# Running the last six spectral modes after all the side work, instead of the last three

## The chip, the cores and the metric

The kernel runs on one core of one Trainium2 chip. The metric is the device time of an execution in microseconds (us), as a median over runs. PE is TensorE, DVE is VectorE, ACT is ScalarE, POOL is GpSimd, SP is SyncE; PEld is the weight load of PE. Times of 0.2% matter in this case, so every variant was timed in five rounds beside the kernel before.

## The reference, cut to what matters

```python
x = attention(q, k, v)                     # 8 batches x 576 rows x 512 columns; half local, half strided heads
X = np.fft.rfft(x, axis=1)                 # cut to 64 modes
Yr = Xr[m] @ w_r[m] - Xi[m] @ w_i[m]       # for each mode m, 512 x 512 weights
Yi = Xr[m] @ w_i[m] + Xi[m] @ w_r[m]
y = np.fft.irfft(Y, n=576, axis=1)
u = x + y
out = u + np.maximum(u @ w_ch, 0.0)        # the channel mix
```

The weights of the modes are 64 x 2 x 1 MB in float32, some 134 MB of the 163 MB that the kernel reads. They are cast to float16 on the way in.

## The kernel before: the parts that matter

The modes run twice over, once for each half of the channels. The second pass, `mode(1, m)`, has "pieces" of other work set between its modes: turns (transposes of the attention's output) and premixes (x @ w_ch, and x put into row order). A `spec` turns the spectra of sixteen finished modes through w_ch. The instructions of PE run in the order in which they are written.

```python
def mode(slot, m):                          # 16 matmuls of 128x128 by 128x16
    ...
    for e in range(4):
        for c in range(4):
            nc.tensor.matmul(yv[:, mi, e, :], wt[pr, XC[c], ds(128 * e, 128)],
                             Xh[half][pr, c, :, :, m], start=(c == 0), stop=(c == 3))
    if m % 2 and (slot or m // 2 not in GUEST):
        w_fetch()                           # a free buffer: the next two modes' weights
    ends = {7: 8}
    if slot and mg == 7:
        ends = {5: 6, 7: 2}                 # the last eight modes are added up as 6 + 2
    ...                                     # after mode 61 and after mode 63: YT = yp + Y0 on DVE
```

```python
work = [...]                                # 4 turns of w_ch, then for each batch 4 turns and 5 premixes: 76
LATE = 10
first = len(work) - 2 * LATE
for m in range(NM - 3):                     # modes 0 to 60
    mode(1, m)
    if m < NM - 3 - LATE:
        upto = -(-first * (m + 1) // (NM - 3 - LATE))
    else:
        upto = first + 2 * (m - (NM - 4 - LATE))     # two pieces a mode
    for w in work[n:upto]:
        w()
    n = upto
    if m >= 16 and m % 16 in (4, 8):
        spec(m // 16 - 1, 0 if m % 16 == 4 else 1)

psum_pools(v=3, u=3)                        # the banks of the pieces become those of the channel mix
...
for i in range(3):                          # five early passes, 512 columns each
    if i < 2:
        v_early(i)
    u_early(i)
warm = psum("v")

def again(n):                               # filler: a matmul whose result nobody reads
    for i in range(n):
        nc.tensor.matmul(warm, idn, v0s[0][:, 2, :], start=True, stop=True)

for m in range(NM - 3, NM):
    mode(1, m)
again(2)
spec_last(0)                                # needs YT of modes 62 and 63: the tail starts here
again(3)
...                                         # v_rows, u_rows for 36 units of 128 rows, and the output
```

The softmax here doesn't subtract the row's maximum and nothing guards it: scores larger than these inputs give would overflow.

## Time and profile before

| what | before |
|---|---|
| time, median of three runs | 436.75 us (436.56 to 436.8) |
| span in the profile | 434.8 us |
| PE busy | 334.7 us, 77% |
| DMA, mean over the span (bytes counted after the cast to float16) | 212 GB/s |
| tail, from `spec_last` (398.0) to the end | 36.8 us |

Two rows of the page for the kernel before, its span in 40 equal slices: the granted clock of PE in tenths of full speed, and the GB/s moved.

```profile
PEclk9999899869895585988885559585769687999999
GB/s 174 210 212 213 214 212 213 211 210 212 214 214 212 214 213 214 214 213 214 214 213 213 213 213 214 214 214 213 213 213 214 213 213 215 213 176 13 268 316 287
```

The transfers run flat at 213 GB/s until slice 35, whatever the clock does: the kernel streams its inputs, weights above all, for 390 us. Slice 36 (391 to 402 us) moves 13 GB/s. There the weights are in and the first output isn't out. This gap is what the change is about.

### The profile page before, as it was taken

The page shows a single profiled execution, that of the slowest core. Times are in us where ns is not written, and L with a number is a line of the kernel's source. Part 1 is how long each engine was busy: PE and PEld are TensorE (multiplying, and loading weights), DVE is VectorE, ACT ScalarE, POOL GpSimd, SP SyncE. Part 2 cuts the span into 40 slices and gives each one's busy share as a digit, 9 for nine tenths or more (in the row PEclk, how much of TensorE's full clock was granted, in tenths as well). Part 3 has the DMA queues.
Part 4 walks back from the last instruction along what each step waited for, and adds up shares of the span by engine and source line. Part 5 has one row for each costly group of instructions (what it writes and reads, how often), then busy time and mean ns, then how long its engine had stood idle before and what let it go on. Part 6 is the DMA issues. An engine that isn't in the chain of part 4 may idle for free.

```text
span 434.8 us, 12063 instructions
## 1 busy us (share of the span) xinstructions
PE 334.7 (77%) x5289; PEld 241.1 (55%) x5289; DVE 215.0 (49%) x466; ACT 188.0 (43%) x353; POOL 129.3 (30%) x208
## 2 busy tenths in 40 slices
PE   1987988789876879787865567679596769888994
PEld 1865776667765666665753345445454445554442
DVE  2788788744452242442511034244335443764895
ACT  1587678635542433534440302113313312443883
POOL 6423332323232222222222222222222222200893
PEclk9999899869895585988885559585769687999999
DMA  8999999999999999999999999999999999980787
GB/s 174 210 212 213 214 212 213 211 210 212 214 214 212 214 213 214 214 213 214 214 213 213 213 213 214 214 214 213 213 213 214 213 213 215 213 176 13 268 316 287
DMA packets 28995, 92.16 MB, mean 212 GB/s; under 512 B 4048, under 2 KB 5072, under 8 KB 28944
## 3 DMA queue, kind: packets, MB, share of 16 engines
q0 software_dynamic: 24704, 81.28, 94.2%
q1 hardware_dynamic: 3440, 9.46, 5.8%
q10 hardware_dynamic: 800, 0.67, 0.6%
q8 instruction: 41, 0.67, 0.6%
q14 instruction: 10, 0.08, 0.0%
HBM read 163.22 MB, written 9.44 MB: 397 GB/s over the span
## 4 chain that ended last, share of the span: by engine, by line
DMA 73%; PE 19%; DVE 2%; issue 2%; ACT 1%; POOL 1%; DVEq 0%; POOLq 0%
DMA wt<-in_moe_w_i_dram 51%; DMA ring<-in_v_dram 7%; DMA ring<-in_k_dram 6%; DMA wt<-in_moe_w_r_dram 4%; DMA ring<-in_q_dram 4%; PE sc L645 3%; PE y L547 3%; PE v L688 2%; PE u L688 2%; PE v L890 2%; PE y L514 1%; PE tp L653 1%; DVE yy L678 1%; PE u L911 1%; DVE xT L597 1%
## 5 line engine op out<-in xcount | busy, mean ns | idle before, releaser
L547 PE MATMUL y<-X,wt 128*128 128x16 f16 (+1 forms) x2048 | 82.4, 192 | 63.5 <-DMA wt<-in_moe_w_i_dram 60.9
L547 PEld LDWEIGHTS <-wt 128*128 128x128 f16 (+1 forms) x2048 | 72.6, 103 | 75.6 <-issue 72.3
L196 POOL DMA_DIRECT2D wt<-in_moe_w_r_dram x62 | 36.5, 589 | 142.2 <-PE y L547 63.1
L196 POOL DMA_DIRECT2D wt<-in_moe_w_i_dram x60 | 35.4, 590 | 70.6 <-DMA wt<-in_moe_w_i_dram 57.9
L654 ACT ACTIVATE v<-sc 128x512 f16<-128x512 f32 x32 | 18.9, 597 | 86.1 <-PE sc L645 86.0
L645 PE MATMUL sc<-w_cp,xT 128*128 128x512 f16 (+1 forms) x160 | 51.3, 450 | 0.4 <-DVE xT L617 0.4
L471 ACT ACTIVATE PL<-sc 128x480 f16<-128x480 f32 (+1 forms) x48 | 27.6, 579 | 47.4 <-PE sc L457 46.9
L655 DVE COPY xo<-tp 128x512 f16<-128x512 f16 x32 | 22.1, 692 | 45.5 <-PE tp L653 45.5
L250 DVE TENSOR_TENSOR xb<-av,rec 90x256 f16<-90x256 f32 (+2 forms) x80 | 36.0, 450 | 2.8
L249 DVE RECIPROCAL rec<-av 90x4 f32<-90x4 f32 (+2 forms) x80 | 14.7, 183 | 42.1 <-PE av L486 31.3
L402 DVE COPY qT<-tp 128x576 f16<-128x576 f16 x16 | 12.0, 758 | 42.8 <-PE tp L395 39.4
L260 ACT ACTIVATE v<-tp 128x640 f16<-128x640 f16 (+1 forms) x24 | 19.4, 808 | 21.2 <-PE tp L429 17.8
L395 PE MATMUL tp<-cI_s,ring 64*64 64x64 f16 x864 | 26.4, 210 | 2.2 <-issue 1.4
L360 ACT ACTIVATE PL<-sc 90x360 f16<-90x360 f32 (+1 forms) x48 | 22.7, 490 | 5.6 <-PE sc L353 4.9
L922 DVE TENSOR_TENSOR osb<-u,rl 128x512 f32<-128x512 f32 x36 | 23.6, 688 | 2.6 <-PE u L688 1.3
L395 PEld LDWEIGHTS <-ring 64*64 64x64 f16 x864 | 20.6, 122 | 7.4 <-issue 4.4
L905 POOL TENSOR_TENSOR rl<-rl,xo 128x512 f32<-128x512 f32 x16 | 18.3, 1156 | 20.5 <-ACT rl L903 20.2
L441 PE MATMUL sc<-cMl_s,cI_s 128*128 128x480 f16 (+1 forms) x48 | 22.4, 467 | 1.6 <-ACT X L260 1.6
L260 ACT ACTIVATE kz<-tp 64x360 f16<-64x360 f16 (+1 forms) x32 | 19.0, 595 | 10.2 <-PE tp L395 8.6
L457 PE MATMUL sc<-qT,kz 128*128 128x160 f16 (+1 forms) x160 | 22.6, 267 | 0.2 <-issue 0.2
L645 PEld LDWEIGHTS <-xT 128*128 128x128 f16 (+1 forms) x160 | 14.5, 109 | 14.6 <-issue 5.7
L285 PE MATMUL tp<-cI_s,ring 72*128 72x72 f16 x256 | 15.1, 206 | 9.5 <-DMA ring<-in_v_dram 8.0
(103 smaller groups left out, 647.8 us busy)
## 6 DMA issues: line engine op xcount, KB each, us to landing
wt<-in_moe_w_r_dram POOLq DMA_DIRECT2D x62, 512.0 KB, 18.9
wt<-in_moe_w_i_dram POOLq DMA_DIRECT2D x60, 512.0 KB, 19.4
out_dram<-osb SPq DMA_DIRECT2D x14, 512.0 KB, 2.7
ring<-in_v_dram POOLq DMA_DIRECT2D x8, 288.0 KB, 13.4
ring<-in_q_dram POOLq DMA_DIRECT2D x8, 288.0 KB, 13.6
ring<-in_k_dram POOLq DMA_DIRECT2D x8, 288.0 KB, 13.2
ring<-in_v_dram POOLq DMA_DIRECT2D x3, 512.0 KB, 15.5
ring<-in_q_dram POOLq DMA_DIRECT2D x3, 512.0 KB, 14.9
```

The source lines that it names most:

```text
L196: nc.gpsimd.dma_start(dst, rows)
L250: nc.vector.tensor_tensor(out=dst, in0=val.rearrange("p h (q c) -> p h c q", c=4), in1=rec[0:n, 0:pieces] .to_broadcast((n, pieces, 64)) . ...
L260: nc.scalar.activation(out=out, in_=in_, func=ACTF.Copy)
L360: nc.scalar.activation(out=PS[0:n, ds(POFF[t], 4 * n)], in_=scp[0:n, 0 : 4 * n], func=ACTF.Exp, scale=SCALE,)
L395: nc.tensor.transpose(tp[ds(64 * hp, 64), ds(64 * i, 64)], qn[ds(64 * hp, 64), ds(64 * (9 * g + i), 64)], idn[ds(64 * hp, 64), ds(64 * hp, ...
L441: nc.tensor.matmul(scp[:, 0 : n * times].rearrange("p (h x) -> p h x", h=times), idn, mask_rows("cMl", n, times), start=True, stop=False,)
L457: nc.tensor.matmul(scp[:, ds(col, n)], kzs[par][:, hp, ds(s0, 128)], qTs[par][:, ds(s0, n)], start=False, stop=(i == len(todo) - 1),)
L471: nc.scalar.activation(out=dst, in_=src, func=ACTF.Exp, scale=SCALE)
L547: nc.tensor.matmul(yv[:, mi, e, :], wt[pr, XC[c], ds(128 * e, 128)], Xh[half][pr, c, :, :, m], start=(c == 0), stop=(c == 3),)
L645: nc.tensor.matmul(vp[pr, :], xT[:, ch, cols], w_chs["cp"][:, ch, :], start=(ch == 0), stop=(ch == 3),)
L655: nc.vector.tensor_copy(out=xo[pr].rearrange("p (h q c) -> p h q c", h=2, c=4), in_=tp[pr, 0:512].rearrange("p (h c q) -> p h q c", h=2, c=4),
L922: nc.vector.tensor_tensor(out=osb[:, t % 2, :], in0=up, in1=rls[b, t][:, t % 2, :], op=AluOp.add)
```

## The change

Its intent: the last six modes, not the last three, are freed of pieces, so that these modes can run as soon as their weights land; the early passes, which need no weights, go between them, and fillers keep PE going. To have all pieces out by mode 57, two pieces a mode begin earlier.

```diff
-    LATE = 10
+    LATE = 12
+    END = NM - 6
     first = len(work) - 2 * LATE
-    for m in range(NM - 3):
+    for m in range(END):
         mode(1, m)
-        if m < NM - 3 - LATE:
-            upto = -(-first * (m + 1) // (NM - 3 - LATE))
+        if m < END - LATE:
+            upto = -(-first * (m + 1) // (END - LATE))
         else:
-            upto = first + 2 * (m - (NM - 4 - LATE))
+            upto = first + 2 * (m + 1 - (END - LATE))
...
-    for i in range(3):
-        if i < 2:
-            v_early(i)
-        u_early(i)
-    warm = psum("v")
...
-    for m in range(NM - 3, NM):
+    early = [lambda i=i: v_early(i) for i in range(2)]
+    early += [lambda i=i: u_early(i) for i in range(3)]
+    warm = psum("v")
+    for m in range(END, NM):
         mode(1, m)
-    again(2)
+        if m < END + 2:
+            for w in early[3 * (m - END) : 3 * (m - END) + 3]:
+                w()
+        else:
+            again(3 if m < NM - 1 else 2)
     spec_last(0)
```

## The prediction

> **What bounds the kernel now.** I read four views in this order: the chain that ended last, cut to 364 to 400 us; the issues of weight transfers with their time to landing, one by one; the timeline of TensorE (PE) from 318 to 372 us; and busy time with granted clock by stretch. The chain comes first, because it says which wait ended last in the only stretch that the change touches, the passage from the second half of the spectral modes to the channel mix. Its columns are start, length and what.
>
> ```profile
> 350.00 18.91 DMA wt<-in_moe_w_i_dram
> ...
> 369.05 0.65 PE y L547 x16
> ...
> 393.02 0.24 PE tp L653 x4
> 393.26 0.02 issue
> 393.28 0.70 DVE xoh L655
> ...
> 394.03 0.39 PE v L890
> ...
> 395.28 0.49 PE y L547 x16
> ...
> 395.86 0.57 DVE YT L575
> ...
> 396.47 1.12 PE y L547 x32
> 397.59 0.43 PE v L952 x2
> 398.02 0.99 PE y L882 x4
> ```
>
> The last transfer on the chain lands at 368.9 us. It carries modes 52 and 53 (each fetch brings two modes, and groups of 16 matmuls of L547 counted back from the last one give the mode numbers). From there to the end the chain is work on the core, not DMA: pieces of turn (L591, L612) and premix (L645, L653), modes, two passes of spec, then the early passes (L890, L911), mode 61 at 395.28, and modes 62 and 63 from 396.47 to 397.59. `spec_last`, which opens the tail, starts at 398.02. So here PE is late. How late is told by the landings of the last two of the eight single-mode transfers, issued at 381.48 and 384.00 (columns: name, queue and operation, count, size, us to landing):
>
> ```profile
> wt<-in_moe_w_i_dram POOLq DMA_DIRECT2D x1, 256.0 KB, 11.7
> wt<-in_moe_w_i_dram POOLq DMA_DIRECT2D x1, 256.0 KB, 9.8
> ```
>
> They land at 381.48 + 11.7 = 393.2 (mode 62) and 384.00 + 9.8 = 393.8 (mode 63). By the same sum modes 58 and 59 are there at 364.34 + 19.4 = 383.7, mode 60 at 371.83 + 15.6 = 387.4 and mode 61 at 374.17 + 14.5 = 388.7. The kernel runs mode 58 at 384.99, 60 at 390.31, and 62 at 396.47: it is behind the weights by 1.3, 2.9 and 3.3 us. In this stretch it falls behind steadily, as it puts two pieces after each mode. That 3.3 us is nearly all that any reordering before the tail can win; it is 0.75% of 436.75.
>
> Then I looked for where PE has room earlier (timeline of PE; in brackets the idle time before and who ended it):
>
> ```profile
> 354.36 0.65 PE L547 MATMUL y<-X,wt 128*128 128x16 f16 x16 [2.41 <-DMA wt<-in_moe_w_i_dram]
> ...
> 359.21 0.64 PE L547 MATMUL y<-X,wt 128*128 128x16 f16 x16 [2.42 <-DMA wt<-in_moe_w_i_dram]
> 359.69 1.87 PE L645 MATMUL sc<-w_cp,xT 128*128 128x512 f16 x4
> ...
> 366.38 1.03 PE L645 MATMUL sc<-w_cp,xT 128*128 128x512 f16 x4
> ```
>
> Before modes 46 and 48 PE stands idle for 2.4 us each, waiting for weights, and afterwards the same four matmuls take 1.87 instead of 1.03 us until about 364.6. The stretches show the clock behind that (PE, PEld, DVE, ACT, POOL busy with counts; then granted clock, DMA share, GB/s):
>
> ```profile
> 351.00:353.00 2.00, 0.94 (x27) 0.80 (x23) 1.63 (x5) 0.00 (x0) 0.59 (x1) 1.00 1.08 217
> 357.00:359.00 2.00, 0.00 (x0) 0.00 (x0) 0.72 (x3) 0.00 (x0) 0.59 (x1) 0.50 1.04 211
> 361.00:363.00 2.00, 2.00 (x24) 1.23 (x23) 0.69 (x1) 0.60 (x1) 0.29 (x1) 0.50 1.05 211
> ```
>
> The clock is 0.50 there, while DMA stays at 211 to 217 GB/s whatever PE does.
>
> **What the Trainium skill says.** "TensorE: Matmul & The Clock Gate", Part 1, says that the array runs at half clock after an idle window of about 3.4 us and at full clock after a busy one. The trace agrees with the halving (0.50 against 1.00), though here a gap of 2.4 us next to sparse work was enough. Part 2 of that page says that matmuls stay in program order and only weight loads are pulled ahead; so a mode queued behind pieces waits for them even when its weights have landed, which the lags of 1.3 to 3.3 us show. "PSUM — Partial Sum Buffer", Terms, forbids two engines in one bank at once; the trace has mode 62 idle for 0.72 us until the add of modes 56 to 61 has left their bank. "DMA: Bandwidth & Descriptors", The descriptor swizzle, gives partitions 64 to 127 to half of the engines; the last transfers, the imaginary weights, go only there, and the DMA share falls from 1.07 to between 0.53 and 0.62 after 388 us. That fixes the landings; the change doesn't touch it.
>
> **The change part by part.** Pieces are the same 76, modes the same 64.
>
> *Moved: six pieces earlier.* By the old formula 58 pieces are done when mode 52 comes, by the new one 64; two after each mode now begin at mode 46, not 51, and all 76 are out after mode 57. A premix costs PE 0.86 + 0.22 = 1.08 us at full clock (chain, L645 and L653), a turn about 0.5 (L591 or L612), a mode 0.49. Between mode 46 and mode 52 come pieces 52 to 63, where it was 52 to 57 with only one turn before mode 48. The pieces now filling the waits are premixes 53 to 55 ahead of mode 48: 3 x 1.08 = 3.2 us at full clock against 2.42 us of idle.
>
> *End of the pieces.* Old: from mode 52 (369.05) to the last piece (393.26) PE takes 24.2 us, with hardly any DMA wait. New, counted from mode 46 (354.36): 24.2, less three modes that go behind the pieces (1.5), plus modes 46 to 51 (6 x 0.49 = 2.9), plus pieces 52 to 57 (0.5 + 5 x 1.08 = 5.9) makes 31.5, so 385.9 at full clock. The idle before mode 46 shrinks only by one turn, so I expect a cold stretch of 3 to 5 us still to follow it, which costs 1.5 to 2.5 us; the end is then near 388.
>
> *The last six modes.* From that end: mode 58 (0.49), beside which most of the 0.77 us wait for the last copy (393.26 to 394.03) passes, the rest 0.3; three early passes (0.65 at 0.22 each); mode 59 (0.49); two (0.43); mode 60 (0.49); three filler matmuls (0.65); mode 61 (0.49); three fillers (0.65, in place of the 0.72 us wait for the add). Sum 4.6: mode 62 could start at 392.6 if the pieces end at 388, at 390.5 if they end at 385.9. Either way its weights land only at 393.2. So modes 62 and 63 become bound by DMA.
>
> *Added on the path.* Mode 62 starts at 393.35 (mode 52 started 0.15 after its landing), ends at 393.84; three fillers take 0.65; mode 63, landed by then, ends at 394.98; two fillers 0.43: `spec_last` at 395.4. The nine new fillers are 9 x 0.22 = 2.0 us of PE, but six lie beside waits; three, 0.65 us, lie on the path. Removed from the path are 398.02 - 395.4 = 2.6 us. The tail, 434.8 - 398.0 = 36.8 us, has the same instructions. 436.75 - 2.6 = 434.15 if all goes well.
>
> **Rivals.**
> 1. *The crowded modes 46 to 57 push PE's lag on to the end.* If the cold stretch lasts until 364 as before, or turns (0.7 to 0.9 us of VectorE each) and the two specs (1.73 us of copies each) stall PE more closely packed, the pieces end at 389.5 and mode 62 starts at 394.1. For it: VectorE is already on the chain between 369.97 and 373.37. Against: those waits are in the 24.2 us already. It would leave 1.8 us of gain, 434.9.
> 2. *Idle before mode 62 cools the clock, and the tail starts at half speed.* If the pieces end at 385.9, PE waits up to 2.7 us less fillers' effect, the length that stood before the cold stretches. A cold stretch of 4 us in a tail where PE is busy 96% (9.64 of 10 us, 400 to 410) costs about 2 us: 436 to 437. Against: PE is dense up to that wait and the fillers stand on both sides of modes 61 to 63.
> 3. *Fetches go out later, as modes free their buffers later.* Mode 51 may be 2 us later. Against: these issues also wait for earlier transfers to complete, and 10 to 19 us lie between issue and landing; a delay of 2 us is absorbed. If not, landings slip by 1 us: 435.2.
> 4. *The last landing isn't the bound and the whole 3 us or more comes:* would need earlier landings; nothing moves bytes. 433.5.
>
> **Range and chances.** I take 434.4: the sum, with a little of rivals 1 and 2. Rival 4 gives the low side, 433.4; rival 2 most of the high side, 436.2. A gain of over 2% would be 8.7 us, more than twice the lag that can be recovered: 1%. A loss of over 2% needs several cold stretches or a broken DMA flow: 1%.
>
> **What would show each step.** Right: mode 62 waits for the imaginary weights near 393.2, that transfer joins the chain, `spec_last` starts near 395.4, the idle of 2.42 us before mode 48 is gone, and the tail still lasts 36.8 us. Wrong: PE has no DMA wait after mode 58 (rival 1); clock below 1.00 and L688 matmuls of twice the length after 394 (rival 2); last landings after 394.5 (rival 3); or the tail's length changes, for which I see no reason.

## The result, and the profile after

The changed kernel takes 434.65 us as a median of four runs (433.94 to 435.15), against 436.77 us (436.56 to 436.91) for the kernel before in the same rounds. The ratio is 0.9951, with a 95% interval of 0.9933 to 0.9968. The prediction was 434.4.

The profiled run took 434.99 us, with a span of 433.2 us. `spec_last` starts at 396.4 instead of 398.0, and the tail is again 36.8 us: all of the 1.6 us between the two traces was won ahead of the tail.

The chain that ended last, of the changed kernel (start, length, what):

```profile
386.51 0.58 ACT zz L260
...
388.92 0.60 ACT v L654
389.52 0.03 issue
389.54 0.60 ACT v0h L654
390.14 0.04 issue
390.19 0.59 PE v L891 x2
...
393.03 0.49 PE y L547 x16
...
393.61 0.57 DVE YT L575
394.18 0.04 issue
394.22 0.64 PE y L547 x16
...
396.42 0.99 PE y L883 x4
```

Modes 62 and 63 are still not on the chain by way of a transfer. Mode 62 at 394.22 waits for the add of modes 56 to 61 on DVE, as before. The last two transfers, issued at 382.25 and 384.70 in this trace, took:

```profile
wt<-in_moe_w_i_dram POOLq DMA_DIRECT2D x1, 256.0 KB, 10.8
wt<-in_moe_w_i_dram POOLq DMA_DIRECT2D x1, 256.0 KB, 9.6
```

So mode 62 was there at 393.05 and mode 63 at 394.3. They ran at 394.22 and 395.34: PE is 1.2 and 1.0 us behind its weights, where it had been 3.3 us behind. The timeline of PE tells where the last microsecond went:

```profile
355.07 0.64 PE L547 MATMUL y<-X,wt 128*128 128x16 f16 x16 [3.14 <-DMA wt<-in_moe_w_i_dram]
...
361.80 0.65 PE L547 MATMUL y<-X,wt 128*128 128x16 f16 x16
...
380.25 1.22 PE L645 MATMUL sc<-w_cp,xT 128*128 128x512 f16 x3 [0.81 <-DVE xT L617]
...
382.21 1.87 PE L645 MATMUL sc<-w_cp,xT 128*128 128x512 f16 x4
```

The lines are modes 46 and 48 and two premixes. Mode 48 (361.80) has no wait left, as foreseen; the wait before mode 46 (355.07) did not shrink but grew, from 2.41 to 3.14 us. Then a premix at 382.21 takes 1.87 us for its four matmuls, the half-speed figure, in a place where the kernel before ran at full clock. The same stretch in both kernels, first before, then after (PE, PEld, DVE, ACT, POOL busy with counts, granted clock, DMA share, GB/s):

```profile
380.00:385.00 5.00, 4.09 (x52) 2.71 (x51) 3.91 (x9) 2.25 (x4) 1.03 (x2) 1.00 1.06 211
```

```profile
380.00:385.00 5.00, 4.75 (x35) 2.53 (x36) 1.64 (x4) 1.19 (x2) 1.11 (x3) 0.66 1.06 211
```

The mean clock is 0.66 instead of 1.00, and PE gets 35 matmuls through in place of 52 (of another mix: the 52 hold more of the short transposes). The question for the experiments was whether the passage is bound by landings (theory A, the prediction) or by the core's own work (theory B, its first rival), and what the clock, the order of the modes and the fillers each do.

### The profile page after: what moved, and what is told of

Its sections match the earlier page's. It is cut to its first block, busy times and chain, and to the rows that moved or that the text cites. A ratio compares the mean times of both kernels' runs of the same rounds, so it can differ in the third digit from the quotient of the medians.

```text
span 433.2 us, 12081 instructions
## 1 busy us (share of the span) xinstructions
PE 337.0 (78%) x5298; PEld 241.4 (56%) x5298; DVE 215.6 (50%) x466; ACT 188.1 (43%) x353; POOL 129.2 (30%) x208
## 4 chain that ended last, share of the span: by engine, by line
DMA 59%; PE 26%; DVE 7%; issue 3%; ACT 3%; POOL 0%; DVEq 0%; POOLq 0%
DMA wt<-in_moe_w_i_dram 48%; DMA wt<-in_moe_w_r_dram 5%; PE y L547 4%; DMA ring<-in_q_dram 4%; PE sc L645 3%; DMA ring<-in_k_dram 2%; PE v L688 2%; PE u L688 2%; PE v L891 2%; PE tp L395 2%; PE sc L514 2%; DVE kz L292 1%; DVE xb L250 1%; PE sc L441 1%; DMA ring<-in_v_dram 1%
## 5 line engine op out<-in xcount | busy, mean ns | idle before, releaser
L645 PE MATMUL sc<-w_cp,xT 128*128 128x512 f16 (+1 forms) x160 | 52.8, 456 | 1.5 <-DVE xT L617 1.5
L655 DVE COPY xo<-tp 128x512 f16<-128x512 f16 x32 | 22.1, 692 | 31.9 <-PE tp L653 31.9
L597 DVE COPY xT<-tp 128x512 f16<-128x512 f16 x16 | 11.0, 689 | 25.6 <-PE tp L591 13.7
```

Of the source, the lines that this page charges most:

```text
L645: nc.tensor.matmul(vp[pr, :], xT[:, ch, cols], w_chs["cp"][:, ch, :], start=(ch == 0), stop=(ch == 3),)
L655: nc.vector.tensor_copy(out=xo[pr].rearrange("p (h q c) -> p h q c", h=2, c=4), in_=tp[pr, 0:512].rearrange("p (h c q) -> p h q c", h=2, c=4),
```

## The experiments

Twelve kernels. The first four ran on one chip (the kernel before: median 437.16 us, 11 runs), the other eight on another (437.01 us, 11 and 12 runs). The landings are worked out from issue and time to landing, as above.

| kernel | time, us | ratio to before | mode 62 landed / ran | mode 63 landed / ran | `spec_last` |
|---|---|---|---|---|---|
| before | 436.75 | 1 | 393.2 / 396.47 | 393.8 / after 62 | 397.98 |
| after | 434.65 | 0.9951 | 393.05 / 394.22 | 394.3 / 395.34 | 396.37 |
| a_again | 434.67 | 0.9938 | 392.9 / 396.26 | 394.1 / 397.38 | 398.36 |
| a_nofill | 435.59 | 0.9963 | 392.2 / 392.91 | 393.5 / after 62 | 394.98 |
| a_even | 435.31 | 0.9961 | 392.8 / 392.91 | 394.0 / 394.18 | 395.51 |
| a_pair | 434.07 | 0.9920 | 390.9 / 392.60 | 393.3 / 393.73 | 394.70 |
| b_old_warm | 437.92 | 1.0016 | 392.2 / 397.33 | 393.4 / after 62 | 398.84 |
| b_warm | 434.21 | 0.9940 | 392.7 / 392.83 | 393.9 / 394.06 | 395.09 |
| b_even_warm | 434.37 | 0.9936 | 392.5 / 392.61 | 393.6 / 393.79 | 394.81 |
| b_even_pair | 434.77 | 0.9945 | 391.5 / 391.60 | 394.0 / 394.14 | 395.17 |
| c_old_even | 434.99 | 0.9951 | 391.9 / 393.75 | 393.2 / after 62 | 395.51 |
| c_lump | 434.02 | 0.9930 | 393.1 / 393.77 | 394.3 / 394.89 | 395.87 |
| c_warm_pair | 433.66 | 0.9929 | 391.3 / 391.42 | 393.8 / 393.94 | 394.97 |
| c_whole | 435.16 | 0.9962 | 393.4 / 393.54 | 393.4 / 394.67 | 395.69 |

The traces are one execution each; the times are medians of five or six runs (of three before, four after), and the profiled run is one of those. All the ratios of variants that gained lie between 0.992 and 0.9963, with intervals of some 0.2% to either side, so most variants can't be told apart by time; the traces must do that. They have an offset of their own: mode 46's weights landed at 354.95 us in the changed kernel and at 354.24 in the kernel before, so differences of 0.7 us between absolute times of two traces mean little.

### a_again: the changed kernel once more

No edit.

> The changed kernel unaltered, for a second trace and as a measure beside its variants. Theory A (landing): modes 62 and 63 start when their imaginary weights land, near 393.1 and 394.3 us. Theory B (late core): the core's own work of pieces and specs reaches mode 62 after the landing; in the first trace it starts at 394.22 against a landing of 393.05. Under B this trace shows again some 1 us between landing and start, and the pieces end after 389; a cold stretch of the clock somewhere between 376 and 386 may be there or not. Time 434.65, within 0.6, ratio to before 0.995.

Measured: 434.67 us (433.92 to 436.97), ratio 0.9938 (0.9914 to 0.9963). The profiled run happened to be the slowest, 436.97 us. Its clock fell twice late, to 0.50 between 369 and 371 us and to 0.50 between 383 and 385, and mode 62 ran 3.4 us after its landing. Theory B holds, and the cold stretch at 380 to 386 was no accident of the first trace. In that run the gain was gone: `spec_last` started at 398.36, against 397.98 in the trace of the kernel before. When the clock falls differs from run to run, and in these two traces the time with it.

### a_nofill: the nine new fillers taken away

```diff
-            again(3 if m < NM - 1 else 2)
+            again(0 if m < NM - 1 else 2)
```

> The nine filler matmuls ahead of modes 61, 62 and 63 taken away, the two after mode 63 kept. Both theories have the landing of mode 63 (394.3) as the floor: spec_last can start at 394.3 + 0.15 + 0.49 + 0.43 = 395.4, against 396.42. Theory B: fillers cost what lies on the path, 0.65 ahead of mode 61 and 0.65 ahead of mode 63, but the landing caps the gain at 1.0 us: 433.6. Theory A in its strict form: only the 0.65 ahead of mode 63 is on the path: 434.0. Theory C (fillers keep the clock up): the granted clock falls below 1.00 between 394 and 402 and the time is 435.5 or more.

Measured: 435.59 us (434.71 to 437.71), ratio 0.9963. Up to `spec_last` the fillers do cost something: from mode 60 to `spec_last` it is 3.8 us (391.18 to 394.98), against 4.6 us (391.74 to 396.37) with them, so 0.8 us of the nine lie on the path. But `spec_last` itself:

```profile
394.98 1.91 PE L883 MATMUL y<-w_ch,YT 128*128 128x512 f16 x4
```

It takes 1.91 us instead of 1.04, and the clock is 0.72 from 393 to 395 and 0.50 from 395 to 397. From `spec_last` to the last matmul it takes 32.0 us (394.98 to 426.97) where the changed kernel takes 30.9 (396.37 to 427.23). This is what theory C expected, and the time of 435.59 agrees: the fillers give back 1.1 us in the tail for 0.8 us ahead of it. By time alone the two kernels aren't apart (434.67 in the same rounds, and the intervals overlap).

### a_even: pieces spread evenly

```diff
-    LATE = 12
+    LATE = 0
```

> LATE = 0: the pieces are spread evenly over modes 0 to 57 (1.31 per mode), none crowded late; 68 of 76 are done when mode 52 comes, instead of 64. Theory B: the core is no longer late, the pieces are all out by 388 and modes 58 to 63 wait for their weights; mode 62 starts within 0.3 us of its landing near 393.1, mode 63 follows after 0.65 of fillers at 394.3 or 394.5, spec_last near 395.5: 433.7. Theory A: the passage is bound by landings already, no gain: 434.6. Theory C: the idle time moves to the last modes, where it cools the clock: below 1.00 after 394 and 436.

Measured: 435.31 us (434.98 to 437.35), ratio 0.9961. The first half of theory B came true (mode 62 ran 0.1 us after its landing, `spec_last` started at 395.51), and the gain was eaten by what theory C had named (timeline of PE):

```profile
392.91 0.64 PE L547 MATMUL y<-X,wt 128*128 128x16 f16 x16 [2.39 <-DMA wt<-in_moe_w_i_dram]
...
395.51 1.91 PE L883 MATMUL y<-w_ch,YT 128*128 128x512 f16 x4
```

Here PE is on time: mode 62 waits for its transfer, and after that wait the clock is at 0.50 for the start of the tail, even with three fillers on each side. From `spec_last` to the last matmul it takes 31.7 us, 0.9 us more than in the changed kernel.

### a_pair: the last transfers in another order

```diff
+            if i >= 2 * NM - 4:
+                for j in range(2):
+                    for ri, src in enumerate((moe_w_r, moe_w_i)):
+                        nc.gpsimd.dma_start(wt[ds(64 * ri, 64), j] ..., src[m + j, ...] ...)
```

(in place of both real modes, then both imaginary ones.)

> The last two fetches in the order real 60, imaginary 60, real 61, imaginary 61, and so on, instead of both reals before both imaginaries: real weights go to partitions 0 to 63 and imaginary ones to 64 to 127, and in the old order the DMA share is halved for the last 6 us (387 to 393). If both halves of the engines finish together, the last landing comes about 3 us earlier, near 391. Theory B: modes start no earlier, since the core is late anyway: 434.6. Theory A: spec_last comes 1.0 us or more earlier (up to 3): 433.6 or less. If the landing doesn't move, the order of the issues isn't what spaces the last transfers.

Measured: 434.07 us (433.42 to 434.49), ratio 0.9920 (0.9901 to 0.9939). The last landing was at 393.3, not near 391: only mode 62 moved up, to 390.9. The DMA share fell to 0.54 between 389 and 391 us as before (0.54), so the uneven order isn't why the last transfers are slow. Mode 62 ran at 392.60, bound by the add once more, so landings weren't its limit here either; the time lies between what theories A and B expected. What sets this trace apart is that its clock didn't fall a second time:

```profile
380.12 0.82 PE L656 MATMUL sc<-w_cp,xT 128*128 128x512 f16 x3 [0.81 <-DVE xT L628]
...
381.48 1.03 PE L656 MATMUL sc<-w_cp,xT 128*128 128x512 f16 x4
...
384.74 0.64 PE L558 MATMUL y<-X,wt 128*128 128x16 f16 x16
```

The instructions from there to mode 57 are those of the changed kernel (lines shifted by 11). Here they take 4.6 us (380.12 to 384.74), there 6.1 us (380.25 to 386.31). A second cold stretch costs 1.4 us.

### b_old_warm: the kernel before, kept warm in its idle time

```diff
+        if m in {43: 4, 45: 8, 47: 8}:
+            fill({43: 4, 45: 8, 47: 8}[m])      # filler matmuls into an idle bank
```

> The kernel before, with 4, 8 and 8 filler matmuls after the pieces of modes 43, 45 and 47, where PE stands idle for weights anyway: 0.9 and 1.7 us each at full clock. Theory D: PE is late at the end because those idle times cool its clock (0.50 from 354.7 to 364.6, which costs some 4 us of PE); kept warm, it reaches modes 62 and 63 about 2 to 3 us earlier and the kernel before gains as much as the change does: 434 to 435. Theory E: the change gains by putting work into the idle time and modes behind the pieces, not by the clock: fillers add no progress, the core is DMA-bound until mode 52 (368.9) whatever the clock before, and the time stays 436.8 or more.

Measured: 437.92 us (437.17 to 438.23), ratio 1.0016. The clock was 1.00 from 351 to 363 us, where the kernel before falls to 0.50 from 355 to 363, and nothing was won (timeline of PE):

```profile
359.06 0.65 PE L547 MATMUL y<-X,wt 128*128 128x16 f16 x16 [0.96 <-DMA wt<-in_moe_w_i_dram]
...
364.01 0.65 PE L547 MATMUL y<-X,wt 128*128 128x16 f16 x16 [1.65 <-DMA wt<-in_moe_w_i_dram]
...
397.33 1.12 PE L547 MATMUL y<-X,wt 128*128 128x16 f16 x32 [0.72 <-DVE YT L575]
```

A faster core only waits for the next weights at 364, after which the clock falls there (0.50 from 365 to 367), and mode 62 is as late as ever. Theory D falls, theory E stands: without pieces to put into the idle time the speed is of no use there. The trace of the kernel before says why: its mode 52 (369.05) still waits 0.20 us for its weights, so no speed won earlier reaches past it. From mode 52 to mode 62 both kernels take 27.4 us (369.05 to 396.47, and 369.89 to 397.33).

### b_warm: the changed kernel, kept warm

```diff
+            if i == 0 and m in {54: 1, 55: 3}:
+                fill({54: 1, 55: 3}[m])         # behind the first piece of these modes
...
+        if m in {43: 4, 45: 12}:
+            fill({43: 4, 45: 12}[m])
```

> The changed kernel with 4 and 12 fillers after modes 43 and 45 and 1 and 3 fillers in the turns of modes 54 and 55. If the cold stretches (355 to 360, and in two of three traces 380 to 386) are what makes the core late by 1 to 3 us, the clock stays at 1.00 in both places in the trace, the pieces end before 388, mode 62 is within 0.3 us of its landing and spec_last starts at 395.5: 433.5, with less scatter between runs than the 433.9 to 437.0 of the unaltered one. If the turns are bound by VectorE copies rather than the clock, the fillers change nothing or cost up to 1 us: 434.7 to 435.7.

Measured: 434.21 us (433.57 to 435.65), ratio 0.9940. In the trace the clock is 1.00 from 355 us to past 415, and now the passage is as the prediction had drawn it:

```profile
392.83 0.64 PE L547 MATMUL y<-X,wt 128*128 128x16 f16 x16 [0.89 <-DMA wt<-in_moe_w_i_dram]
...
394.06 0.64 PE L547 MATMUL y<-X,wt 128*128 128x16 f16 x16
...
395.09 1.04 PE L892 MATMUL y<-w_ch,YT 128*128 128x512 f16 x4
```

Mode 62 waits 0.89 us for its weights, and `spec_last` starts at 395.1, against 395.4 in the prediction. So the cold stretches are what put the unaltered changed kernel behind; the two later kernels with the same fillers, c_warm_pair and c_whole, also have PE on time in their traces. The expected 433.5 did not come: the time is better than the unaltered kernel's only within the scatter, and the range of six runs, 2.1 us against 3.1, is too little to call the scatter smaller. One trace can't show what the slower runs (435.25 and 435.65) met.

### b_even_warm and b_even_pair: even spread, with the waits filled

```diff
-            again(3 if m < NM - 1 else 2)
+            again({60: 3, 61: 12, 62: 3, 63: 2}[m])      # b_even_warm, on a_even
+            again({60: 3, 61: 5, 62: 8, 63: 2}[m])       # b_even_pair, on a_even and a_pair
```

> LATE = 0 as before in this study, but 12 fillers instead of 3 ahead of mode 62, into the 2.39 us in which PE waited there and after which the clock fell to 0.50 for 3 to 4 us. Theory C (that idle time is what the even spread loses by): the clock stays at 1.00 after 393, spec_last starts at 395.5 as there but takes 1.04 instead of 1.91 us, and the time falls by about 2 us, 435.3 to 433.4. If it stays above 435, the tail's loss had another cause.

> Even spread, paired order of the last transfers and 3, 5 and 8 fillers ahead of modes 61, 62 and 63. The paired order brought mode 62 to land at 390.9 and mode 63 at 393.3. With the core on time, mode 62 runs at 391, mode 63 at 393.5, spec_last starts at 394.4 and the clock stays up: 432.5. If landings weren't what binds once the core is on time, it equals the even spread with 12 fillers.

Measured: 434.37 us (433.91 to 434.54), ratio 0.9936, and 434.77 us (434.36 to 435.12), ratio 0.9945. In b_even_warm `spec_last` starts at 394.81, takes 1.04 us, and the clock is 1.00 from 379 us to 415: with nine more fillers ahead of mode 62 what a_even had lost is back, as theory C expected. It is one trace against one: in c_whole, below, a wait as long as that of a_even, with three fillers, was not followed by a fall, and the intervals of the two ratios overlap. The expected 2 us came out as 0.9 of median, partly because the time from the last matmul to the end was 6.7 us in this trace. It was long in all four kernels of this call (6.3 to 6.7 us), and 5.9 to 6.0 in all other traces. The last output transfer took 4.3 us to land here instead of 3.1 to 3.3. Why isn't known. b_even_pair missed its 432.5 and is no better than b_even_warm, since mode 63's weights, and not mode 62's, were the last to come: it ran at 394.14 after a wait of 0.17.

### c_old_even: one number changed in the kernel before

```diff
-    LATE = 10
+    LATE = 0
```

> The kernel before with LATE = 0 and nothing else: its 76 pieces spread evenly over modes 0 to 60, the last three modes bare and the early passes in one lump as before, no new fillers. Theory F: what the change gains is only that work no longer piles up late, and the order of the last six modes adds nothing; then this edit alone brings mode 62 to within 0.3 us of its landing near 393.2 and the time to 434 or less. Theory G: the six bare modes are needed; then mode 62 starts after 394 and the time is 435.5 or more. Theory C (idle time before mode 62 cools the clock) can spoil the gain in either case: clock below 1.00 after 393.

Measured: 434.99 us (434.35 to 435.78), ratio 0.9951 (0.9935 to 0.9967). That is the ratio of the whole change.

```profile
393.75 1.12 PE L547 MATMUL y<-X,wt 128*128 128x16 f16 x32 [0.72 <-DVE YT L575]
...
395.51 1.91 PE L882 MATMUL y<-w_ch,YT 128*128 128x512 f16 x4
```

`spec_last` starts 2.5 us earlier than in the kernel before, with three bare modes as ever. The 1.91 us show that the clock had fallen (0.50 from 395 to 397): from `spec_last` to the last matmul it takes 31.9 us (395.51 to 427.44) instead of 30.9, so 1.1 us went back that way. The waits ahead of it, 0.79 and 0.72 us, are those of the kernel before, whose clock stayed at 1.00 there. The numbers of both theories failed: mode 62 came 1.8 us after its landing and the time is not 434 or less (theory F), but mode 62 started before 394 and the time is under 435.5 (theory G). What the run does show is that work no longer piling up late is enough for a gain as large as that of the change, without the six bare modes.

### c_lump: the early passes in one lump after mode 60

```diff
-        if m < END + 2:
-            for w in early[3 * (m - END) : 3 * (m - END) + 3]:
-                w()
-        else:
+        if m == END + 2:
+            for w in early:
+                w()
+        if m >= END + 2:
             again(3 if m < NM - 1 else 2)
```

> The changed kernel with its five early passes in one lump after mode 60 instead of between modes 58 and 60; fillers and pieces unaltered. The waits for the last copies (0.36 us in the first trace of after) would then lie beside three modes instead of one: 0.3 us less at best, so 434.3 to 434.7. If the early passes between the modes earn something of their own, it is slower than 435.

Measured: 434.02 us (433.68 to 434.48), ratio 0.9930 (0.9917 to 0.9943). Modes 58 to 60 run without a break at 389.24, the first early pass follows at 390.68 with no wait, and `spec_last` is at 395.87. Setting early passes between the modes earns nothing; the lump is as fast or a little faster. The interval overlaps that of the changed kernel.

### c_warm_pair and c_whole: what is left at the floor

```diff
+            again({60: 3, 61: 3, 62: 5, 63: 2}[m])       # c_warm_pair: b_warm and a_pair
-                elif i < 2 * NM - 4:
+                elif i < 2 * NM:                         # c_whole: b_warm, all fetches whole
```

> The changed kernel with fillers in the idle time of modes 43 and 45 and in the turns, as before in this study, with the paired order of the last transfers and 5 fillers ahead of mode 63. Core on time and mode 62 landed at 390.9: mode 62 starts at 391.9, mode 63 at 393.5 when it lands, spec_last at 394.4, and the time is 433.5: better than 434.21 by up to 0.7. If it's no better, mode 63's landing is the floor for all of them.

> The changed kernel with the same fillers, and the last two fetches in transfers of two modes like all others (512 KB), not cut by mode. If the DMA share falls to half after 387 because the last transfers are small and few in flight, it stays near 1.05 longer and the last landing comes 1 to 3 us earlier, near 391 to 392.5: time 433 or less. If it falls for another reason, modes 62 and 63 land together at 393.5 to 394, and the time is 434.2 or up to 0.6 more.

Measured: 433.66 us (433.6 to 434.72), ratio 0.9929, and 435.16 us (434.44 to 436.94), ratio 0.9962. In c_warm_pair both modes run within 0.2 us of their landing. Whole transfers land no earlier, both at 393.4 (374.22 + 19.2), and the DMA share falls to 0.52 between 389 and 391 there too. So neither the order nor the size of the last transfers makes the rate halve after 387 us; what does is open. The landings of a_pair narrow it down: its last four transfers land at 389.6, 390.9, 392.1 and 393.3, real and imaginary in turn, about 1.25 us apart. 256 KB in 1.25 us would be 210 GB/s, but between 389 and 391 only 109 GB/s moved. So about half of each must have moved before (an estimate from these numbers), as if one half of the queue's work, for transfers of either kind, ran some 6 us behind the other.

c_whole also bears on theory C (timeline of PE):

```profile
393.54 0.64 PE L547 MATMUL y<-X,wt 128*128 128x16 f16 x16 [2.42 <-DMA wt<-in_moe_w_i_dram]
...
395.69 1.04 PE L892 MATMUL y<-w_ch,YT 128*128 128x512 f16 x4
```

A wait of 2.42 us behind three fillers, and yet the clock stayed at 1.00 in this trace. Its profiled run was among its two fastest (434.44); the median is above the 434.8 that was allowed for, and what its slow runs (436.48 and 436.94) met isn't recorded.

c_warm_pair has the lowest median of all, 3.35 us under the kernel before, but its interval (0.9913 to 0.9945) overlaps that of the unaltered change (0.9914 to 0.9963 in a_again), so it can't be called faster than that one.

## Why the prediction was right, and where it wasn't

**Time.** 434.4 was predicted and 434.65 measured, a gain of 2.1 us (436.77 - 434.65) where 2.35 was foreseen. That the number came so close is in part luck: the sum alone gave 434.15, some allowance for rivals 1 and 2 was added to it, and the path then failed in one step, which put `spec_last` 1.0 us later than summed in the trace (396.4, not 395.4).

**The bound on the gain** held. The prediction said that the 3.3 us by which PE lagged its weights is nearly all that can be won. The largest gains among the twelve kernels were 3.1 us (437.16 - 434.07, a_pair) and 3.35 us (437.01 - 433.66, c_warm_pair), both with the landing order altered too.

**Pieces into idle time** held: the wait of 2.42 us before mode 48 is gone, and the tail has its 36.8 us. b_old_warm shows that it had to be pieces, and not speed, that filled it. Two details were misread. Seven pieces (51 to 57), not six, lie between modes 46 and 52 in the kernel before, and two turns, not one, between modes 46 and 48. And the wait before mode 46, which was to shrink by a turn, grew: 3.14 us here, 2.8 to 3.2 in a_again, a_nofill, a_pair and c_lump. It cost nothing, as up to mode 46 both kernels wait for the stream.

**"So modes 62 and 63 become bound by DMA"** is the step that failed in the kernel as it stands. Its rival 1 came true: mode 62 waits for the add, not for its weights, 1.2 us after the landing. The terms that were mis-sized are the end of the pieces, put near 388, and the way from there to mode 62, put at 4.6 us. The pieces ended at 389.25 (the last transposes, 388.86 + 0.39). Of these 1.25 us, 0.7 is that mode 46, from which the sum starts, ran at 355.07 and not at 354.36; the rest is that 34.2 us of work followed where 33.6 had been allowed. The sum allowed for one cold stretch, and there was a second one at 380 to 384, which cost 1.4 us by the comparison with a_pair. From the end of the pieces to mode 62 it took 5.0 us. Half of the excess came before the first early pass, which waited for ACT, whose copies of the second `spec` stood ahead of those of the last premixes; the other half at the add, which held mode 62 until 0.88 us after mode 61, where three fillers of 0.65 were to cover it. In a_pair, without the second cold stretch, the pieces ended at 387.7 and mode 62 ran at 392.60, where the prediction's sum had 388 and 392.6. Where fillers took the cold stretches away (b_warm), the mechanism appeared as drawn: mode 62 waited 0.89 us for its transfer, and `spec_last` stood at 395.1.

**The fillers** were put at 0.65 us on the path. Without them 0.8 us was won ahead of the tail and 1.1 us lost in it, so the size was about right, and their use was one that the prediction gave only as an argument against rival 2.

**Rival 2**, a cool start of the tail, did not come in the kernel as it stands, but in the traces of a_nofill, a_even and c_old_even. There it cost 0.9 to 1.1 us of tail, less than the 2 us in the prediction. That idle time causes it isn't shown: c_whole left PE idle as long as a_even did, and the kernel before has the same waits as c_old_even (0.79 and 0.72 us), and in neither did the clock fall. Counted over all traces, the tail began below full clock in one of ten with fillers ahead of modes 61 to 63, and in two of four without.

**Rival 3** did not come: the fetches went out up to 3 us later around mode 49 (365.63 against 362.71), and the last landing moved by 0.5 us, from 393.8 to 394.3, less than the 0.7 us by which mode 46's weights were already late in this trace.

**The reading of the last transfers** was wrong in its cause. It held that the imaginary weights, which come last, go to half of the engines, and took that from a page's account of another shape of transfer. With real and imaginary transfers in turn (a_pair) the rate halved at the same time. The share was also read too narrowly: in the kernel before it is 0.62 to 0.54 from 388 to 391, and 0.44 from 391 to 393.

**Which part earns the gain.** Four kernels answer it by ratio. With the late crowding and three bare modes it is 1 (before); with pieces spread evenly and three bare modes 0.9951 (c_old_even); with pieces crowded but out six modes early 0.9951 and 0.9938 (the change); with both 0.9961 (a_even). So either is enough, and both together give no more, as far as these intervals tell. The early passes between modes earn nothing (c_lump, 0.9930). Fillers keep the clock up where PE must wait in the traces of b_warm and b_even_warm; a gain in time from them alone isn't clear of the noise in any pair of kernels here.

## What to carry to other kernels

When an engine that runs in order is late at the end of a stream, measure how late each of its last consumers is against the landing of its own data: that lag, and not the busy share, was about the most that a new order won here (3.3 us of lag, 3.35 us at best). Spread side work over the stream rather than crowding it near the end; in these runs it cost nothing where the engine would have waited for the stream anyway. Once PE is on time it has to wait, so try fillers in the waits just ahead of dense work, and look at the clock there in more than one trace.

## What the Trainium skill lacked or had wrong

- "TensorE: Matmul & The Clock Gate" ties the fall of the clock to idle gaps of about 3 us or more and calls the window free-running. In these traces gaps of 0.32 and 0.81 us between short transposes were enough at 376 to 380 us (clock 0.50 from 381 to 383, with PE shown 82% busy, 4.12 of 5.00 us, just before), and the same instructions didn't cool it in a_pair. A wait of 2.39 us was followed by a fall in a_even, and one of 2.42 us with the same three fillers ahead of it wasn't in c_whole. A gap's length alone doesn't foretell it; the free-running window would fit this scatter, but no run here tested it. The page isn't silent on this: it also says that short, frequent idles between groups of matmuls make the clock go up and down ("A second HAM failure mode"), and that transposes don't count as busy in the same way (Part 4). The late falls in the changed kernel, a_again, a_nofill and c_lump all come just after turns, which are transposes, so they fit both; the rule of 3 us is what falls short.
- The same page has nothing on filler matmuls inside a kernel. Here, with 12 fillers of 0.22 us each in a wait of 2.4 us, the clock stayed at 1.00 into dense work (b_even_warm against a_even: `spec_last` took 1.04 us, not 1.91; but c_whole stayed at 1.00 with three), and nine cost 0.8 us where the path didn't wait.
- No page that I found has it that a queue of weight transfers falls to half its rate for the last 6 us before it runs empty (DMA share 1.07 to some 0.54 from 387 us on), alike for three orders and sizes of the last transfers. "DMA: Bandwidth & Descriptors", The descriptor swizzle, from which the prediction took a cause, describes a transfer to 128 partitions and refers to another section for other shapes. It isn't wrong by this; the prediction applied it to transfers to 64 partitions, and a_pair did not bear that out.
